# Second stage in two passes of four units, first batch's units ahead of the second product, and VectorE in GpSimd's place for early weight tiles

## The chip, the cores and the metric

The kernel runs on one core of a Trainium2 chip. The metric is the device time of one execution in microseconds. Of the core's engines TensorE (PE; its weight loads are shown as PEld) multiplies, VectorE (DVE) and ScalarE (ACT) work on tiles, GpSimd (POOL) does a part of the weight conversion, and SP issues most DMAs from one queue that is in order.

## The reference

Three layers in a row: an attention over 32 memory slots, a gated feed-forward (silu) and a feed-forward with an ELU.

```python
a = softmax(phi, axis=seq)                        # 8 batches, 8 heads, 576 x 32
k_m, v_m = a.T @ k, a.T @ v                       # 32 x 64 a head
attn = softmax(q @ k_m.T / 8)                     # 576 x 32
x = concat_heads(attn @ v_m)                      # 4608 tokens x 512
g, val = x @ w_gate, x @ w_val                    # 1536 columns each
x = (silu(g) * val) @ w_out                       # 4608 x 512
h = x @ w_in                                      # 2048 columns
out = where(h > 0, h, exp(min(h, 0)) - 1) @ w_out2
```

## The kernel before

**Numbers.** The weights come as 64-bit floats. `load_w` brings a tile of 128 x 512 of them to the chip (SP, 512 KB) and turns it into 32-bit floats: one ScalarE pass, four VectorE passes (L101, L102, L104, L105), and then GpSimd. With `split` (all `wo` and `w2` tiles) the tile becomes a high and a low half for products of three matmuls, with one ScalarE pass and two GpSimd passes (L108, L109); without (the `wg` tiles) one GpSimd pass (L111) adds the correction. After the first units exist, a conversion's VectorE passes are ordered behind the last one's `h` (L98).

**Stage one** (L392) goes over 8 batches, each in two halves of 288 tokens. The gate and value weights are multiplied with the batch's 32-slot `v_m` first: `vw(b, p)` (16 small matmuls, two ScalarE and two VectorE passes) makes the tile `VW[b, p]` for units 2p and 2p + 1, from four `wg` tiles of group p. A unit is 128 columns of the hidden layer: `gate1` (6 matmuls, L151 to L153), `val1` (6 matmuls, VectorE's `h` in L183, then halves `hh` and `hl` in L162 and L164). Stage one does units 0 to 3 (`UA = 4`); `down1` multiplies them with `wo` 0 to 3, four groups of 12 matmuls, and ScalarE stores the partial sum as `p1_d` in DRAM. Between the units, `tick()` issues pieces of a `todo` list in step with the number of ticks: the attention of later batches (`front_tasks`, `back_tasks`), weight tiles, and the next batch's `vw`. In the first batch these are the conversions of `wo` 0 to 3 and the attention of batches 1 and 2. In the last batch they are `load2(0)`, `wg` groups 4 and 5, `wo` 7 to 11, `vw(0, 2)` and `vw(0, 3)`. The attention result of each batch is also stored as `at_d`.

**Stage two** (L501) goes over the 8 batches again, two halves each, units 4 to 11 in each half. `at2` is read back from `at_d` (`load2`, two buffers). `down2` adds a unit into four PSUM banks `acc0` to `acc3` (one buffer each), two units late (`LAG = 2`). After the half's last unit VectorE adds the four banks to the tile `p1` that was read from `p1_d` (L475), and SP stores it as `x1_d`. The tile `p1` has one buffer, so the next half's `p1` is loaded when this store has landed. During hf 1 the four `vw` of the next batch are made, into four buffers of `vx`. 19 of the 32 `w2` tiles are converted here: one each in 11 halves, eight in the last batch.

**Stage three** (L577) goes over 9 blocks of 512 tokens with 16 units of 24 matmuls; the other 13 `w2` tiles are converted behind its first 13 units.

**Order.** All instructions are traced in this order, and a scheduler with a timeline model then sets the order on each engine's queue, earlier traced work first where both are ready in its model. `tc.issue_after(x)` keeps what is traced inside behind `x` on x's engine. On the chip each queue is in order.

Of the kernel before, what the change touches and what calls it, by code (L numbers as in the profile page):

```python
# [26 lines left out]
UA = 4  # L27
NCH = 5
NWA = 24
NWB = 16  # L30
NWE = 14
NWC = 10
NKV = 5
NQ = 3

# [2 lines left out]
def attention_moe_moe(ctx: ExitStack, tc: tile.TileContext, qT, phiT, kv, kv4, w1g, w1o, w2, out):  # L38
# [31 lines left out]

    at_d = [dram.tile([128, 2, 2, S], F32R, name=f"atd{b}") for b in range(B)]
    p1_d = [dram.tile([128, KD, S], F32, name=f"p1d{b}") for b in range(B)]
    x1_d = [dram.tile([128, KD, S], F32, name=f"x1d{b}") for b in range(B)]

    last = {}
# [7 lines left out]
                call()  # L83


    def load_w(store, u, i, src, pool, split=True):
        raw = wr_p.tile([128, 512, 2], I32, tag="wr", name="wr")
        nc.sync.dma_start(out=raw, in_=src.rearrange("p (n t) -> p n t", t=2))
        lo32, hi32 = raw[:, :, 0], raw[:, :, 1]
        if split:  # L90
            hi = pool.tile([128, 512], F32R, tag="w", name="whi")
            lo = pool.tile([128, 512], F32R, tag="w", name="wlo")
        else:
            full = pool.tile([128, 512], F32, tag="w", name="wg")
        v = wt_p.tile([128, 512], F32, tag="wv", name="wv")
        c = wt_p.tile([128, 512], I32, tag="wc", name="wc")
        vi, cf = v.bitcast(I32), c.bitcast(F32)
        with tc.issue_after(last["h"].ins) if "h" in last else nullcontext():  # L98

            act(out=v, in_=hi32.bitcast(F32), func=AF.Copy, scale=2.0 ** -112)  # L100
            nc.vector.tensor_scalar(out=c, in0=vi, scalar1=3, scalar2=None, op0=ALU.logical_shift_left)  # L101
            stt(out=vi, in0=vi, scalar=-2 ** 31, in1=c, op0=ALU.bitwise_and, op1=ALU.bitwise_or)  # L102

            nc.vector.tensor_scalar(out=c, in0=vi, scalar1=-2 ** 23, scalar2=None, op0=ALU.bitwise_and)  # L104
            stt(out=cf, in0=lo32.bitcast(U32), scalar=2.0 ** -52, in1=cf, op0=ALU.mult, op1=ALU.mult)  # L105
            if split:
                act(out=hi, in_=v, func=AF.Copy)
                nc.gpsimd.tensor_tensor(out=v, in0=v, in1=hi.bitcast(F32), op=ALU.subtract)  # L108
                nc.gpsimd.tensor_tensor(out=lo, in0=v, in1=cf, op=ALU.add)  # L109
            else:  # L110
                nc.gpsimd.tensor_tensor(out=full, in0=v, in1=cf, op=ALU.add)  # L111
        store[u][i] = (hi, lo) if split else full


# [4 lines left out]
    def load_wg(p, k, pool):  # L119
        load_w(WG, p, k, w1g[p, k], pool, False)  # L120

    def load_wo(u, pool):
        load_w(WO, u, 0, w1o[u], pool)

    def load_w2(u, i, pool):
        load_w(W2, u, i, w2[u, :, i * 1024:(i + 1) * 1024], pool)
# [19 lines left out]
    def up1(ps, w, c0, at, s0):  # L146
        cs, ss = slice(c0, c0 + 128), slice(s0, s0 + HS)
        for g in range(2):
            wh, wl = w[:, 0, g, cs], w[:, 1, g, cs]
            ah, al = at[:, 0, g, ss], at[:, 1, g, ss]  # L150
            mm(ps, lhsT=wh, rhs=ah, start=g == 0, stop=False)  # L151
            mm(ps, lhsT=wh, rhs=al, start=False, stop=False)  # L152
            mm(ps, lhsT=wl, rhs=ah, start=False, stop=g == 1)  # L153

    def down(ps, w, hs, ms, start, stop):
        mm(ps, lhsT=w[0][:, ms], rhs=hs[0], start=start, stop=False)  # L156
        mm(ps, lhsT=w[1][:, ms], rhs=hs[0], start=False, stop=False)  # L157
        mm(ps, lhsT=w[0][:, ms], rhs=hs[1], start=False, stop=stop)  # L158
# [208 lines left out]
    for k in range(KD):  # L367
        load_wg(1, k, wa_p)
    load(Bs[1])
    vw(0, 1, G2)  # L370

    def down1(b, hf, hs, m):
        ps = ps_gv.tile([128, HS], F32, tag="g", name="pd")
# [10 lines left out]
        at2[b] = av_p.tile([128, 2, 2, S], F32R, tag="at", name="at2")  # L384
        nc.sync.dma_start(out=at2[b].bitcast(F32), in_=at_d[b].bitcast(F32))


    def wg_tasks(p):
        return [lambda k=k: load_wg(p, k, wa_p) for k in range(KD)]

    prev = None
    for b in range(B):  # L392
        todo = []
        bk = list(back_tasks(b + 1)) if b + 1 < B else []
        fr = list(front_tasks(b + 2)) if b + 2 < B else []
        if b == 0:
            wo = [lambda u=u: load_wo(u, wa_p) for u in range(UA)]
            f1 = [lambda: (Bs[1].phi(), load_q(Bs[1]))] + list(front_tasks(1)) + [lambda: Bs[2].phi()]
            for i in range(max(len(wo), len(f1))):
                todo += wo[i:i + 1] + f1[i:i + 1]  # L400
        if 1 <= b <= 4:
            bk += [lambda k=k, p=2 + (b - 1) // 2: load_wg(p, k, wa_p) for k in (0, 1) if b % 2] + \
                [lambda k=k, p=2 + (b - 1) // 2: load_wg(p, k, wa_p) for k in (2, 3) if b % 2 == 0]
        if b == B - 2:
            wb_p = ctx.enter_context(tc.tile_pool(name="wb", bufs=NWB))
            ps_vw = ctx.enter_context(tc.tile_pool(name="ps_vw", bufs=1, space=PSUM))
            V2 = [(ps_vw, "vw"), (ps_gv, "g")]
            fr += [lambda u=u: load_wo(u, wb_p) for u in (4, 5, 6)]
        if b == B - 1:
            fr.append(lambda: load2(0))  # L410
            fr += wg_tasks(4) + [lambda: load_wo(7, wb_p), lambda: vw(0, 2, V2), lambda: load_wo(8, wb_p)]
            fr += wg_tasks(5) + [lambda: load_wo(9, wb_p), lambda: vw(0, 3, V2), lambda: load_wo(10, wb_p),
                                 lambda: load_wo(11, wb_p)]
        for i in range(max(len(bk), len(fr))):
            todo += fr[i:i + 1] + bk[i:i + 1]
        if b + 1 < B:
            todo += vw_tasks(b + 1)
        done = [0, 0]
        spread = 18 if b == 0 else 16 if b < B - 2 else 24

        def tick():
            done[0] += 1
            upto = min(len(todo), -(-len(todo) * (done[0] + 3) // spread))
            while done[1] < upto:
                todo[done[1]]()
                done[1] += 1

        silu = b == B - 1
        tick()
        for hf in range(2):  # L430
            hs = []
            for u in range(UA):
                s = gate1(b, u, Bs[b].at, HS * hf, silu)
                tick()
                hs.append(val1(b, u, Bs[b].at, HS * hf, s, silu))
                tick()
                if prev:
                    down1(*prev, u)
                    tick()
            prev = b, hf, hs  # L440
        while done[1] < len(todo):
            tick()
        if b == B - 3:
            st_fr.close()
            st_ps.close()
# [12 lines left out]
    def more_w2(pool, n=1):  # L458
        for _ in range(n):
            load_w2(*todo2.pop(0), pool)  # L460

    def load_p1(b, hf):
        t = p1_p.tile([128, KD, HS], F32, tag="p1", name="p1l")
        nc.sync.dma_start(out=t, in_=p1_d[b][:, :, HS * hf:HS * hf + HS])
        return t

    def down2(q):
        b, hf, u, hs, accs, p1 = q
        if u == UA:
            accs += [ps_acc.tile([128, HS], F32, tag=f"acc{m}", name=f"acc{m}") for m in range(KD)]  # L470
        for m in range(KD):
            down(accs[m], WO[u][0], hs, slice(128 * m, 128 * m + 128), u == UA, u == NU1 - 1)
        if u == NU1 - 1:
            for m in range(KD):
                tt(out=p1[:, m, :], in0=accs[m], in1=p1[:, m, :], op=ALU.add)  # L475
            nc.sync.dma_start(out=x1_d[b][:, :, HS * hf:HS * hf + HS], in_=p1)

    def load3(j):
        xt = []
# [14 lines left out]

    LAG = 2
    pend = []
    for p in (4, 5):
        vw(0, p, V2)
    w2q = [wa_p] * 4 + [we_p] * 7 + [wa_p] * 8
    vwq = []  # L500
    for b in range(B):  # L501
        for hf in range(2):
            p1 = load_p1(b, hf)
            accs = []
            if hf == 0 and b + 1 < B:
                load2(b + 1)
            for u in range(UA, NU1):
                s = gate1(b, u, at2[b], HS * hf, True)
                pend.append((b, hf, u, val1(b, u, at2[b], HS * hf, s, True), accs, p1))
                if len(pend) > LAG:  # L510
                    down2(pend.pop(0))
                if vwq:
                    vw(*vwq.pop(0), V2)
                if hf == 1 and u % 2 == 1 and b + 1 < B:
                    vwq.append((b + 1, u // 2))
                elif hf == 1 and u == 7 and b == B - 1:
                    nxt = load3(0)
                if u % 2 == 1 if b == B - 1 else u == 8 and len(w2q) > 8:
                    more_w2(w2q.pop(0))
    for q in pend:  # L520
        down2(q)
    pend = []
    st_p1.close()
    st_r.close()
    wc_p = ctx.enter_context(tc.tile_pool(name="wc", bufs=NWC, side="right"))
    w2q = [wb_p] * 8 + [wc_p] * 5
    h3_p = ctx.enter_context(tc.tile_pool(name="h3", bufs=4, side="right"))
    t3_p = ctx.enter_context(tc.tile_pool(name="t3", bufs=2, side="right"))

# [95 lines left out]
```

## Time and profile before

| | |
|---|---|
| median of 3 runs | 1608.3 us (1608.15 to 1608.68) |
| the profiled execution: own time, span | 1609.44 us, 1607.6 us |
| TensorE matmuls busy | 1533.4 us, 95% |
| VectorE busy | 988.0 us, 61% |
| ScalarE, GpSimd busy | 654.0 us, 166.2 us |
| mean granted TensorE clock | 0.981 |
| first matmul of stage one's first unit | 55.5 us |
| first matmul of stage two, last of it | 361.2 us, 810.0 us |

The span runs from the first to the last instruction; the own time has some 1.8 us around it. A busy TensorE is not one at its peak, since its matmuls are pipelined, so the windows below are read with their counts. The shares are means over stages that differ: in the first stage VectorE is nearly full at some places, in the second and third it is about half busy.

### The profile page before, as it was taken

The numbers are of one execution on the slowest core, as the hardware profiler recorded it, in microseconds if no ns is written. First come the engines' busy times: TensorE is split into PE (matmuls) and PEld (weight loads), VectorE is DVE, ScalarE is ACT, GpSimd is POOL, SyncE is SP. The second block draws the span as 40 slices with busy tenths as digits, with TensorE's granted clock in tenths as the row PEclk, the third lists the DMA queues.
The fourth block names the chain that finished last, engine by engine and source line by source line (L and its number), as shares of the span: only waits on it lengthen the run. The fifth ranks groups of instructions, "written<-read, shape, count | busy, mean of one in ns | idle before, by whom it ended". The sixth has DMA issues, their size and how long they took to land.

```text
span 1607.6 us, 24193 instructions
## 1 busy us (share of the span) xinstructions
PE 1533.4 (95%) x9816; PEld 1311.5 (82%) x9816; DVE 988.0 (61%) x1702; ACT 654.0 (41%) x1249; POOL 166.2 (10%) x119
## 2 busy tenths in 40 slices
PE   3599999979999999999998999999999999999998
PEld 2478789769999999999976788888888888888887
DVE  7997876795444454435889755555555555555554
ACT  3455444543333333333544433334343434343333
POOL 1400010241101011000435100000000000000000
PEclk7799999999999999999999999999999999999999
DMA  8887332452322232211522101001010101010000
GB/s 346 293 307 265 109 112 75 170 192 72 106 77 82 73 102 86 73 60 45 157 85 74 53 1 45 9 6 48 1 53 0 53 0 53 1 53 1 27 1 27
DMA packets 62961, 136.32 MB, mean 85 GB/s; under 512 B 6528, under 2 KB 37248, under 8 KB 60800
## 3 DMA queue, kind: packets, MB, share of 16 engines
q1 hardware_dynamic: 53632, 125.32, 22.7%
q10 hardware_dynamic: 9216, 9.44, 1.7%
q8 instruction: 77, 1.26, 0.3%
q14 instruction: 36, 0.29, 0.1%
HBM read 96.99 MB, written 37.75 MB: 84 GB/s over the span
## 4 chain that ended last, share of the span: by engine, by line
PE 81%; DVE 14%; DMA 2%; issue 2%; ACT 1%; SPq 0%; POOL 0%; ACTq 0%; DVEq 0%; POOLq 0%
PE acc L565 7%; PE acc L564 7%; PE acc L566 7%; PE pu L538 7%; PE pu L539 7%; PE pu L540 7%; PE acc L156 4%; PE acc L157 4%; PE acc L158 4%; PE pg L151 3%; PE pv L151 3%; PE pv L153 3%; PE pg L153 3%; PE pv L152 3%; PE pg L152 3%; PE pvw L139 3%
## 5 line engine op out<-in xcount | busy, mean ns | idle before, releaser
L538 PE MATMUL pu<-x1s,whi 128*128 128x512 f32 x576 | 224.7, 390 | 2.5 <-DVE g L554 2.5
L564 PE MATMUL acc<-whi,hh 128*128 128x512 f32 x576 | 224.5, 390 | 2.1 <-ACT hh L162 2.1
L566 PE MATMUL acc<-whi,hl 128*128 128x512 f32 x576 | 222.4, 390 | 3.3 <-DVE hl L164 3.3
L540 PE MATMUL pu<-x1s,wlo 128*128 128x512 f32 x576 | 224.8, 390 | 0.0
L539 PE MATMUL pu<-x1s,whi 128*128 128x512 f32 x576 | 224.7, 390 | 0.0
L565 PE MATMUL acc<-wlo,hh 128*128 128x512 f32 x576 | 224.2, 389 | 0.0
L553 DVE SCALAR_TENSOR_TENSOR g<-e,g 128x512 f32<-128x512 f32 x144 | 107.5, 747 | 157.5 <-ACT g L552 157.5
L162 ACT ACTIVATE hh<-g 128x512 fp32r<-128x512 f32 x144 | 91.0, 632 | 216.9 <-DVE g L554 216.9
L551 ACT ACTIVATE e<-g 128x512 f32<-128x512 f32 x144 | 90.8, 631 | 210.0 <-DVE g L550 210.0
L183 DVE SCALAR_TENSOR_TENSOR h<-s,pv 128x288 f32<-128x288 f32 x192 | 86.5, 451 | 140.8 <-PE pv L153 118.6
L164 DVE TENSOR_TENSOR hl<-g,hh 128x512 fp32r<-128x512 f32 x144 | 99.9, 694 | 88.3 <-ACT hh L162 88.2
L156 PE MATMUL acc<-hh,whi 128*128 128x288 f32 x512 | 151.0, 296 | 0.0
L157 PE MATMUL acc<-hh,wlo 128*128 128x288 f32 x512 | 150.6, 294 | 0.0
L158 PE MATMUL acc<-hl,whi 128*128 128x288 f32 x512 | 149.4, 295 | 0.0
L162 ACT ACTIVATE hh<-h 128x288 fp32r<-128x288 f32 x192 | 85.1, 443 | 138.9 <-DVE h L183 137.2
L164 DVE TENSOR_TENSOR hl<-h,hh 128x288 fp32r<-128x288 f32 x192 | 97.0, 505 | 63.0 <-ACT hh L162 62.8
L550 DVE TENSOR_SCALAR g<-pu 128x512 f32<-128x512 f32 x144 | 99.1, 689 | 55.2 <-PE pu L540 51.8
L566 PEld LDWEIGHTS acc<-whi,hl 128*128 128x128 f32 x576 | 108.0, 188 | 28.4 <-DVE hl L164 6.1
L151 PE MATMUL pg<-at,vw 128*128 128x288 f32 x384 | 119.4, 311 | 10.4 <-DVE vw L144 6.0
L564 PEld LDWEIGHTS acc<-whi,hh 128*128 128x128 f32 x576 | 108.3, 188 | 25.4 <-ACT hh L162 3.0
L538 PEld LDWEIGHTS pu<-x1s,whi 128*128 128x128 f32 x576 | 108.3, 188 | 25.3 <-DVE g L554 2.9
L539 PEld LDWEIGHTS pu<-x1s,whi 128*128 128x128 f32 x576 | 108.5, 188 | 22.6
(87 smaller groups left out, 3187.9 us busy)
## 6 DMA issues: line engine op xcount, KB each, us to landing
kvr<-kv SPq DMA_DIRECT2D x32, 512.0 KB, 7.9
wr<-w SPq DMA_DIRECT2D x32, 512.0 KB, 3.6
wr<-w1g SPq DMA_DIRECT2D x24, 512.0 KB, 4.9
qr<-qT SPq DMA_DIRECT2D x16, 576.0 KB, 5.9
atd<-at SPq DMA_DIRECT2D x8, 1152.0 KB, 5.3
p1d<-p ACTq DMA_DIRECT2D x64, 144.0 KB, 2.0
p1l<-p1d SPq DMA_DIRECT2D x16, 576.0 KB, 4.1
at<-atd SPq DMA_DIRECT2D x8, 1152.0 KB, 5.2
```

The lines of the kernel that those rows point to most:

```text
L151: mm(ps, lhsT=wh, rhs=ah, start=g == 0, stop=False)
L156: mm(ps, lhsT=w[0][:, ms], rhs=hs[0], start=start, stop=False)
L157: mm(ps, lhsT=w[1][:, ms], rhs=hs[0], start=False, stop=False)
L158: mm(ps, lhsT=w[0][:, ms], rhs=hs[1], start=False, stop=stop)
L162: act(out=hh, in_=h, func=AF.Copy)
L164: tt(out=hl, in0=h, in1=hh.bitcast(F32), op=ALU.subtract)
L538: mm(ps, lhsT=wh[:, k, :], rhs=xh, start=k == 0, stop=False)
L539: mm(ps, lhsT=wh[:, k, :], rhs=xl, start=False, stop=False)
L540: mm(ps, lhsT=wl[:, k, :], rhs=xh, start=False, stop=k == KD - 1)
L564: mm(accs[c], lhsT=hs[0][:, cs], rhs=wh, start=u == 0, stop=False)
L565: mm(accs[c], lhsT=hs[0][:, cs], rhs=wl_, start=False, stop=False)
L566: mm(accs[c], lhsT=hs[1][:, cs], rhs=wh, start=False, stop=u == NU2 - 1)
```

## The change

1. Stage two becomes two passes over all batches: units 4 to 7 with `p1_d` in and a new `p2_d` out, then units 8 to 11 with `p2_d` in and `x1_d` out. A half has four units; there are 32 halves instead of 16, `at` is read back 16 times instead of 8, and each batch of a pass needs two `vw`.
2. A list `conv` holds 34 conversions for stage two, one for each half (two in each of the last two): `wg` groups 4 and 5, `wo` 8 to 11, 22 `w2` tiles. The last batch of stage one keeps `wo` 7 only, and `vw(0, 4)`, `vw(0, 5)` are made during the first pass. Stage three converts 10 tiles. The pools' sizes follow (`NWB` 16 to 8, `NWE` 14 to 20, `NWC` 10 to 12).
3. `vw(0, 1)` is traced behind the first batch's second unit instead of ahead of the loop. In the first batch the `todo` list starts four ticks later (`-1` for `+3`), and what it issues on TensorE is kept behind the last `up1`.
4. In `load_w` the last additions run on VectorE instead of GpSimd for all `wg` tiles and for `wo` 0 to 3.

```diff
-                nc.gpsimd.tensor_tensor(out=v, in0=v, in1=hi.bitcast(F32), op=ALU.subtract)
-                nc.gpsimd.tensor_tensor(out=lo, in0=v, in1=cf, op=ALU.add)
+                part = tt if own else nc.gpsimd.tensor_tensor
+                part(out=v, in0=v, in1=hi.bitcast(F32), op=ALU.subtract)
+                part(out=lo, in0=v, in1=cf, op=ALU.add)
             else:
-                nc.gpsimd.tensor_tensor(out=full, in0=v, in1=cf, op=ALU.add)
+                tt(out=full, in0=v, in1=cf, op=ALU.add)
...
-        load_w(WO, u, 0, w1o[u], pool)
+        load_w(WO, u, 0, w1o[u], pool, own=u < UA)
...
-            mm(ps, lhsT=wl, rhs=ah, start=False, stop=g == 1)
+            last["pe"] = mm(ps, lhsT=wl, rhs=ah, start=False, stop=g == 1)
...
-    vw(0, 1, G2)
...
-            fr += wg_tasks(4) + [lambda: load_wo(7, wb_p), lambda: vw(0, 2, V2), lambda: load_wo(8, wb_p)]
-            fr += wg_tasks(5) + [lambda: load_wo(9, wb_p), lambda: vw(0, 3, V2), lambda: load_wo(10, wb_p),
-                                 lambda: load_wo(11, wb_p)]
+            fr += [lambda: load_wo(7, wb_p), lambda: vw(0, 2, V2), lambda: vw(0, 3, V2)]
...
-            upto = min(len(todo), -(-len(todo) * (done[0] + 3) // spread))
+            upto = min(len(todo), -(-len(todo) * (done[0] + (3 if b else -1)) // spread))
             while done[1] < upto:
-                todo[done[1]]()
+                with nullcontext() if b else tc.issue_after(last["pe"].ins):
+                    todo[done[1]]()
                 done[1] += 1
...
+                if (b, hf, u) == (0, 0, 1):
+                    vw(0, 1, G2)
...
+    conv = [lambda p=p, k=k: load_wg(p, k, wa_p) for p in (4, 5) for k in range(KD)] + \
+        [lambda u=u: load_wo(u, wa_p) for u in range(2 * UA, NU1)] + \
+        [lambda pool=pool: more_w2(pool) for pool in [we_p] * 10 + [wa_p] * 4 + [wb_p] * 4 + [wa_p] * 4]
...
+    for ps, (src, dst) in enumerate(((p1_d, p2_d), (p2_d, x1_d))):
+        for b in range(B):
+            nb, np_ = (b + 1, ps) if b + 1 < B else (0, ps + 1)
+            for hf in range(2):
+                p1 = load_p1(b, hf, src)
+                accs = []
+                if hf == 0 and np_ < 2:
+                    load2(nb)
+                for u in range(UA * (ps + 1), UA * (ps + 2)):
+                    s = gate1(b, u, at2[b], HS * hf, True)
+                    pend.append((b, hf, u, val1(b, u, at2[b], HS * hf, s, True), accs, p1, dst))
+                    if len(pend) > LAG:
+                        down2(pend.pop(0))
+                    if vwq:
+                        vw(*vwq.pop(0), V2)
+                    if hf == 1 and u % 2 == 1 and np_ < 2:
+                        vwq.append((nb, u // 2 + UA // 2 * (np_ - ps)))
+                    elif hf == 1 and u == 9 and np_ == 2:
+                        nxt = load3(0)
+                    if u % (2 if np_ == 2 else 4) == 1:
+                        conv.pop(0)()
...
-    w2q = [wb_p] * 8 + [wc_p] * 5
+    w2q = [wa_p] * 4 + [wc_p] * 6
```

## Rows read from the trace of the kernel before

**Rows 1.** The page's busy times, and TensorE in 40 slices of 40.2 us

```profile
PE 1533.4 (95%) x9816; PEld 1311.5 (82%) x9816; DVE 988.0 (61%) x1702; ACT 654.0 (41%) x1249; POOL 166.2 (10%) x119
...
PE   3599999979999999999998999999999999999998
```

**Rows 2.** Windows by stage; the columns stand in the first line

```profile
core 0: us, PE busy (x) PEld busy (x) DVE busy (x) ACT busy (x) POOL busy (x), PEclk, DMA share, GB/s
20.00:55.50 35.50, 15.17 (x159) 6.83 (x159) 35.09 (x60) 13.67 (x28) 10.64 (x8) 0.55 0.90 340
20.00:104.20 84.20, 54.58 (x602) 36.88 (x602) 83.23 (x154) 39.41 (x86) 19.77 (x14) 0.76 0.83 308
104.20:144.50 40.30, 39.21 (x441) 33.20 (x440) 31.28 (x67) 22.87 (x54) 2.56 (x2) 1.00 0.74 266
313.80:361.20 47.40, 38.31 (x298) 32.84 (x296) 45.77 (x69) 23.63 (x50) 21.35 (x15) 0.99 0.62 208
361.20:367.30 6.10, 6.06 (x27) 4.55 (x27) 5.85 (x8) 3.48 (x8) 3.70 (x4) 0.54 0.36 111
472.10:527.80 55.70, 55.70 (x451) 51.71 (x450) 26.18 (x57) 20.15 (x44) 6.29 (x4) 1.00 0.27 84
750.70:810.00 59.30, 59.30 (x443) 57.55 (x443) 45.03 (x85) 27.01 (x57) 22.65 (x16) 1.00 0.42 133
819.40:890.00 70.60, 65.40 (x272) 51.66 (x273) 69.51 (x96) 34.84 (x57) 36.82 (x24) 0.98 0.20 68
975.00:1060.00 85.00, 85.00 (x376) 70.38 (x375) 46.81 (x69) 33.08 (x53) 0.00 (x0) 1.00 0.08 25
```

**Rows 3.** Chain of waits in order of time: start us, us, what

```profile
395.35 1.02 PE pvw L139 x16
```

**Rows 4.** Waits of TensorE from 313.8 to 372 us: total, times, longest

```profile
PE pg L151 <- DVE vw L144: 5.7, 2, 3.5
...
PE pvw L139 <- ACT p L377: 1.4, 1, 1.4
```

**Rows 5.** VectorE's groups by line and shape, 367 to 750 us

```profile
L164 DVE TENSOR_TENSOR hl<-h,hh 128x288 fp32r<-128x288 f32 x111 | 51.7, 466 | 49.1 <-ACT hh L162 49.0
...
L475 DVE TENSOR_TENSOR p1l<-acc,p1l 128x288 f32<-128x288 f32 x52 | 21.2, 450 | 0.0
...
L102 DVE SCALAR_TENSOR_TENSOR wv<-wv,wc 128x512 int32<-128x512 int32 x11 | 7.6, 693 | 0.4
```

**Rows 6.** Timeline of VectorE at a change of half: start us, us

```profile
783.70 0.45 DVE L475 TENSOR_TENSOR p1l<-acc,p1l 128x288 f32<-128x288 f32 x1
...
786.60 0.45 DVE L475 TENSOR_TENSOR p1l<-acc,p1l 128x288 f32<-128x288 f32 x1
```

**Rows 7.** Timeline of SP's DMA queue, 410 to 430 us

```profile
414.95 0.33 SPq L385 DMA_DIRECT2D at<-atd  x1
...
424.92 0.55 SPq L476 DMA_DIRECT2D x1d<-p1l  x1
...
428.23 0.54 SPq L464 DMA_DIRECT2D p1l<-p1d  x1
```

**Rows 8.** DMA issues: KB each, median us from issue to landing

```profile
p1l<-p1d SPq DMA_DIRECT2D x16, 576.0 KB, 4.1
...
at<-atd SPq DMA_DIRECT2D x8, 1152.0 KB, 5.2
```

**Rows 9.** VectorE's groups by line and shape, 12 to 80 us

```profile
L102 DVE SCALAR_TENSOR_TENSOR wv<-wv,wc 128x512 int32<-128x512 int32 x12 | 11.9, 994 | 0.2
...
L164 DVE TENSOR_TENSOR hl<-h,hh 128x288 fp32r<-128x288 f32 x2 | 2.8, 1416 | 0.0
```

**Rows 10.** Timeline before the first unit: start us, us, what

```profile
34.29 0.65 DVE L144 TENSOR_TENSOR vw<-pvw,vw 128x512 fp32r<-128x512 f32 x1
...
35.34 0.76 DVE L308 TENSOR_TENSOR at<-ex,at 128x576 fp32r<-128x576 f32 x1
...
55.50 0.61 PE L151 MATMUL pg<-at,vw 128*128 128x288 f32 x1
```

## What was predicted, before the changed kernel ran

> **What bounds the kernel now.** I read the page first, then the windows by stage, then TensorE's waits in the windows where it is not full. TensorE is busy 1533.4 of 1607.6 us, and the digits of its slices fall below 9 at the left edge, in the ninth slice (322 to 362 us) and a little in the one from 844 us [rows 1]. So what there is to win stands in three places, and the rest has to stay as full as it is.
>
> The windows say how much [rows 2]. A batch of the steady second stage, 472.1 to 527.8 us, has TensorE at 55.70 of 55.70 us for 451 records, 448 by the code. Of these 64 are four `vw` products at 1.02 us each [rows 3], so 384 matmuls take 55.7 - 4.1 = 51.6 us, 0.134 us each; that is my yardstick for 288 columns. In the third stage 376 matmuls take 85.0 us, 0.226 us each.
>
> - *The last batch of stage one, 313.8 to 361.2 us.* VectorE is busy 45.77 of 47.40 us, TensorE 38.31. TensorE has 298 records; with four `vw` taken off (56 records are in the trace) some 242 matmuls are left. Work: 242 x 0.134 + 4 x 1.02 = 36.5 us. Lost: 10.9 us. In 361.2 to 367.3 the granted clock is 0.54, that is nearly all at the lower of its two levels (1.2 GHz, after the 3.5 us wait for `vw`), and 27 records that are worth at most 3.6 us take 6.1: another 2.5. What TensorE waits for is VectorE's `vw` [rows 4], which stands behind weight tiles 4 and 5 in VectorE's queue.
> - *The ramp of stage three, 819.4 to 890.* VectorE 69.51 of 70.60 us; 272 matmuls x 0.226 = 61.5 us, so 9.1 us are lost while 13 weight tiles are turned into halves, 0.70 us a tile.
> - *The start.* Between 20 and 104.2 us VectorE is busy 83.2 of 84.2 us and TensorE 54.6; the clock of 20 to 55.5 is 0.55.
>
> **The change, part by part.**
>
> *Tiles taken out of the last batch.* Eight `wg` tiles (groups 4 and 5), `wo` 8 to 11 and the products `vw(0,4)`, `vw(0,5)` leave the todo list of batch 7 and the lines behind it. Only `wo` 7, `load2(0)`, `vw(0,2)` and `vw(0,3)` stay. With VectorE no longer full, the batch should take what TensorE needs. Of 10.9 + 2.5 = 13.4 us I leave 1 for `wo` 7 and for hand-overs: -12.4 us. The two products are not saved, they run in stage two. Bounds: nothing, if another wait takes their place, and -13.4.
>
> *The same tiles in stage two.* All 34 conversions are now one a half (two a half in the last batch). VectorE is busy 26.18 of 55.70 us a batch there [rows 2], so it has 29 us free for each 55.7. It gets 15 tiles more than before (34 against 19) and 64 more additions of `p1` at 0.450 us [rows 5], 28.8 us. A tile's four passes take at most 4 x 0.69 = 2.8 us [rows 5], say 4 with what GpSimd's neighbourhood adds. That is some 90 us over eight old batches that have 236 free. Cost: 0 as long as that cover holds. The cover at the tight place, the change of half, is seen in the last old batch: there conversions, four additions and `load3` mix on VectorE, the additions end within 3.4 us [rows 6], and TensorE has 59.30 of 59.30 us in 750.7 to 810 [rows 2]. Without it, each late addition holds `acc0`, and the next `down2` waits behind it.
>
> *The doubled round of `p1`.* Each half is now 4 units, 4 x 24 x 0.134 = 12.9 us, and `p1` still has one buffer. The round is: additions (4 x 0.45 = 1.8 us), store, then the load that SP may issue only when the store has landed (3.3 us from issue to issue), then 4.1 us to landing [rows 7, 8]: 9.2 us against 12.9, so 3.7 us of slack where there were 16.5. SP gets 16 stores, 16 `p1` loads and 8 loads of `at` more. A store stands at the head of SP's queue until its additions are done, so the weight loads and the `at` load behind it wait too; each is asked for a half or more ahead. Cost 0; from the other side, if the 5.2 us of an `at` load [rows 8] came whole between store and reload, the round would be 14.4 us and a half would wait 1.5 us. The second pass reads `p2` 16 halves after it was stored, so nothing waits there.
>
> *Stage three.* 22 tiles are ready instead of 19, 10 remain: -3 x 0.70 = -2.1 us. Bounds 0 and -4, the latter if the last units catch up at the steady rate. The pools behind it (12 instead of 10 buffers in `wc`, still released by the last store) move nothing on the path. `load3(0)` is asked for two units before the end of the last half instead of four, but its `vx` buffers come free earlier; 0.
>
> *The start: VectorE's additions.* 16 GpSimd instructions of the first 100 us (one for each of 8 `wg`, two for each of 4 `wo`) become VectorE passes. The trace has no such pass; the nearest row is the two-input pass of the same size, 0.693 us [rows 5], so +11.0 us on a full engine. Against it: a VectorE pass beside a running GpSimd one is stretched. In 12 to 80 us the 12 passes of L102 mean 994 ns against 693 undisturbed, the two of L164 1416 against 466 [rows 5, 9]: 3.6 + 1.9 = 5.5 us from these two lines alone, which is the least, since others of its lines can be stretched in the same way. Net 0 to +5.5 us of VectorE, and each tile is ready sooner by GpSimd's longer time. I take +1 on the path, bounds -3 and +11.
>
> The Trainium skill, Perfetto Trace Analysis, section Optimizing Scalar/DVE Operations, advises moving work off a saturated VectorE, GpSimd included, which speaks against this edit; by that alone the sum would be 10 us worse. The same section adds that the two share a read port, so that moving between them might not help, and the stretched rows agree with that part.
>
> *The start: order.* `vw(0,1)` moves from ahead of the loop to behind unit 1, and the first batch's tasks start four ticks later, with their TensorE instructions behind the last `up1`. Now the first `pg` matmul runs at 55.50 us, behind the second `vw`, although the halves of `vw(0,0)` end at 34.9 and `at` at 36.1 [rows 10]. So two units, 24 matmuls, can move into a stretch in which TensorE idles: 3.2 us at 0.134, 6.4 at the lower clock. I take -5. Bounds: 0, if VectorE, which is full to 104 us, only trades this for a later batch 1; and the whole 19.4 us between 36.1 and 55.5, which VectorE could only pay for from its slack in batch 1 (31.28 of 40.30 us, 9 us free [rows 2]), so -10 is as far as I go. What waits behind: TensorE's queue is in order, so batch 1's transposes, products and scores, which VectorE waits for, stand behind the first `up1` until about 38 us.
>
> **Sum.** -12.4 - 2.1 + 1 - 5 = -18.5 us. The profiled execution's span is 1607.6 and its own time 1609.44 us, 1.1 above the median of 1608.3. So a span of 1589.1, an own time of 1590.9, a median of 1589.8; I say 1590.
>
> **The rivals.**
> 1. *The reload of `p1` becomes the bound (slower).* Place: every change of half in stage two. It decides once the round exceeds 12.9 us, and it costs more than the gain from 0.6 us a half on (18.5 over 31 halves). With the `at` load between store and reload in each of 16 batch passes it is 16 x 1.5 = 24 us, so 1590 + 24 = 1614. For it: one buffer, one queue. Against: the old `at` load went out at 414.95, ten us ahead of the store at 424.92 [rows 7].
> 2. *The start gets worse.* Deferred tasks make batch 1's attention late, or the 11 us of additions land on the path: +10 instead of -4, 1604. For it: VectorE has 1 us free in 84. Against: the stretched rows.
> 3. *The start gains far more*, as VectorE's slack of batches 1 and 2 is used: -14 instead of -4, 1580.
> 4. *The change doesn't do what it says for batch 7*: the batch stays slow, since the down products' copies (`p`, ACT) hold `ps_gv`; one 1.4 us wait of that kind stands beside 5.7 us of VectorE's [rows 4]. Half the 12.4 is lost: 1596.
>
> **How the numbers follow.** Forecast (1584 to 1595 of its own) 0.52; rival 3 0.15; rival 4 0.11; rival 2 0.11; rival 1 0.11. A difference under 0.2% (3.2 us) can't be told from none. Rival 1 is slower in most of its reach, and a bad case of 2 comes to no change: faster 0.85, same 0.04, slower 0.11. The range leaves out the far half of rival 3 and most of rival 1: 1577 to 1604.
>
> **What would show it.** Right: the last batch of stage one takes about 36 us with VectorE below half; stage two has TensorE full and 55.7 us for eight units' pairs; no wait of a `down2` on L475's additions; the first `pg` starts near 38 us and batch 1 near 99; the ramp shows 10 tiles. Wrong: `acc` matmuls waiting for additions or for `p1l` at the changes of half, a wait of `p1`'s additions on its load, low clock inside stage two, or batch 1 starting behind 104 us.

## The result, and the profile after

The changed kernel takes 1585.95 us (median of 4 runs, 1584.58 to 1587.06); the ratio to the kernel before is 0.9855, 95% interval 0.9838 to 0.9872. That is 22.5 us less, where 18.5 were forecast and the range was 1577 to 1604. The profiled execution has a span of 1584.9 us (own time 1587.06), 22.7 less than before. Where the 22.7 us stand, by the same marks in both traces:

| stretch | before, us | after, us | difference | forecast |
|---|---|---|---|---|
| first instruction to the first `pg` of batch 7 | 313.8 | 303.8 | -10.0 | -4 |
| batch 7, to the first `pg` of stage two | 47.4 | 34.4 | -13.0 | -12.4 with what follows |
| stage two, to its last `acc` matmul | 449.0 | 448.8 | -0.2 | 0 |
| the rest | 797.4 | 797.9 | +0.5 | -2.1 |

Some 2 of the 10.0 us at the start are not the change's. They stand in batch 3, which took 35.0 us before, with 6.8 us of it at TensorE's lower clock, and 32.9 after, without. Two traces of the experiments below (two buffers for `p1`, and late tasks only) have the same 6.8 us in that batch, and it takes 35.7 and 35.8 us there; with the whole start undone but no fall of the clock it takes 33.2. So this loss comes and goes from one execution to the next.

The page of the changed kernel, the lines that answer to [rows 1]: busy times, TensorE in 40 slices, and the granted clock.

```profile
PE 1523.7 (96%) x9816; PEld 1307.8 (83%) x9816; DVE 1013.3 (64%) x1798; ACT 649.6 (41%) x1249; POOL 113.4 (7%) x87
...
PE   4699999999999999999989999999999999999998
...
PEclk7899999999999999999999999999999999999999
```

The 7 in the ninth slice is gone. The edge at the left has a slice of 6 instead of 5, and the dip behind the stage change is still there. The windows, which answer to [rows 2]:

```profile
core 0: us, PE busy (x) PEld busy (x) DVE busy (x) ACT busy (x) POOL busy (x), PEclk, DMA share, GB/s
...
20.00:87.60 67.60, 45.57 (x457) 32.61 (x458) 65.21 (x137) 33.60 (x72) 0.00 (x0) 0.76 0.80 288
87.60:134.20 46.60, 42.58 (x495) 34.16 (x493) 41.49 (x92) 24.85 (x57) 0.00 (x0) 1.00 0.85 305
303.80:338.20 34.40, 34.40 (x275) 32.39 (x274) 11.97 (x25) 15.57 (x34) 3.12 (x2) 1.00 0.37 129
...
445.60:501.30 55.70, 55.70 (x450) 51.70 (x449) 37.32 (x72) 21.34 (x48) 10.46 (x8) 1.00 0.50 166
...
797.70:857.00 59.30, 55.08 (x223) 43.40 (x224) 58.21 (x79) 27.96 (x46) 30.87 (x20) 0.95 0.16 54
```

- Batch 7 (third row): VectorE 11.97 us where it had 45.77, TensorE full.
- Stage two (fourth row, two batches of a pass, the same work as one old batch): 55.70 us and 450 records as before; VectorE went from 26.18 to 37.32 us inside it and nothing of that shows.
- The ramp (last row): VectorE is full for 10 tiles now, and 59.3 - 223 x 0.226 = 8.9 us are lost, where 13 tiles had cost 9.1. The clock is part of both: 5.8 us of this window are at the lower level, worth up to 2.9 us, and 3.4 us of the window before, worth up to 1.7. That leaves 6.0 us for 10 tiles and 7.4 for 13, some 0.6 us a tile in both kernels.

The forecast's claim on VectorE's additions can be read off directly. VectorE's groups of the changed kernel in 12 to 80 us, which answer to [rows 5, 9]:

```profile
L103 DVE SCALAR_TENSOR_TENSOR wv<-wv,wc 128x512 int32<-128x512 int32 x12 | 8.1, 684 | 0.1
...
L166 DVE TENSOR_TENSOR hl<-h,hh 128x288 fp32r<-128x288 f32 x7 | 3.1, 450 | 0.4 <-ACT hh L164 0.4
...
L110 DVE TENSOR_TENSOR wv<-wv,whi 128x512 f32<-128x512 f32 x4 | 2.7, 682 | 0.0
```

L103 is the old L102: 684 ns instead of 994. L166 is the old L164: 450 instead of 1416. The added passes take 0.68 us each, as costed.

The round of `p1` in stage two was costed at 9.2 us. SP's queue in one short half (a half without `vw`), the median landing of the second pass's reloads and the landing of this one, and VectorE's first two additions behind it:

```profile
566.76 0.54 SPq L476 DMA_DIRECT2D p2d<-p1l  x1
569.13 0.33 SPq L89 DMA_DIRECT2D wr<-w  x1
570.69 0.55 SPq L463 DMA_DIRECT2D p1l<-p2d  x1
```
```profile
p1l<-p2d SPq DMA_DIRECT2D x16, 576.0 KB, 5.5
...
p1l<-p2d SPq DMA_DIRECT2D x1, 576.0 KB, 5.2
```
```profile
576.66 0.81 DVE L475 TENSOR_TENSOR p1l<-acc,p1l 128x288 f32<-128x288 f32 x2
```

Issue to issue is 3.9 us here (3.3 to 3.5 us at most of the other changes of half) and the landing 5.2 us: the tile is there at 575.9, 0.8 us ahead of the addition. Over the 14 changes that end a short half, the last one left out, the reload is 0.5 to 2.6 us early, 1.1 in the median; at the long ones it is 3.5 to 5.0 us early. Each term of the round but one is longer than costed: the four additions take 2.5 us instead of 1.8, and the landing is 5.3 us in the median of both passes instead of 4.1. With 3.4 us from issue to issue that is a round of 11.2 us, in a short half of 12.4.

At the end of stage two it isn't enough. The chain of waits of the changed kernel, start and length:

```profile
778.60 3.71 DMA x1d<-p1l
...
782.33 5.44 DMA p1l<-p2d
...
787.89 1.56 DVE p1l L475 x4
...
789.47 3.29 DMA x1d<-p1l
...
792.89 1.30 DVE g L553 x2
```

Behind the last unit no other unit's matmuls lengthen the half, so the additions wait 1.6 us for the reload. Then stage three's first `g` waits for the store, since its pool takes the memory that `p1` leaves. It did so in the kernel before, for as long (first line below, 3.42 us); what is new is the reload ahead of it. TensorE waits 4.9 us there, where it was 2.5 (second line before, third after):

```profile
814.59 1.29 DVE L550 TENSOR_SCALAR g<-pu 128x512 f32<-128x512 f32 x2 [3.42 <-DMA x1d<-p1l]
...
PE pu L538 <- DVE g L554: 2.5, 1, 2.5
...
PE pu L541 <- DVE g L557: 4.9, 1, 4.9
```

The clock falls to its lower level (1.2 GHz) there, for 6.8 us where it was 3.4. This difference is no sign of the change: of the six traces of experiments 1 and 2, whose code is the same at this place, three have 3.4 us and three 6.8.

### The profile page after: what moved, and what is told of

Read it like the earlier page. It is cut to its first block, busy times and chain, and to the rows that moved or that the text cites. A ratio compares the mean times of both kernels' runs of the same rounds, so it can differ in the third digit from the quotient of the medians.

```text
span 1584.9 us, 24325 instructions
## 1 busy us (share of the span) xinstructions
PE 1523.7 (96%) x9816; PEld 1307.8 (83%) x9816; DVE 1013.3 (64%) x1798; ACT 649.6 (41%) x1249; POOL 113.4 (7%) x87
## 4 chain that ended last, share of the span: by engine, by line
PE 84%; DVE 11%; DMA 3%; issue 1%; ACT 1%; SPq 0%; ACTq 0%; DVEq 0%
PE acc L567 8%; PE acc L568 8%; PE acc L569 8%; PE pu L543 8%; PE pu L541 8%; PE pu L542 8%; PE acc L158 4%; PE acc L160 4%; PE acc L159 4%; PE pg L153 3%; PE pv L153 3%; PE pg L155 3%; PE pv L155 3%; PE pv L154 3%; PE pg L154 3%; PE pvw L141 3%
## 5 line engine op out<-in xcount | busy, mean ns | idle before, releaser
L164 ACT ACTIVATE hh<-g 128x512 fp32r<-128x512 f32 x144 | 91.0, 632 | 216.1 <-DVE g L557 213.1
L166 DVE TENSOR_TENSOR hl<-g,hh 128x512 fp32r<-128x512 f32 x144 | 99.5, 691 | 90.0 <-ACT hh L164 89.9
L164 ACT ACTIVATE hh<-h 128x288 fp32r<-128x288 f32 x192 | 84.8, 442 | 125.5 <-DVE h L185 124.1
L166 DVE TENSOR_TENSOR hl<-h,hh 128x288 fp32r<-128x288 f32 x192 | 98.1, 511 | 52.3 <-ACT hh L164 52.3
L543 PEld LDWEIGHTS pu<-x1s,wlo 128*128 128x128 f32 x576 | 108.6, 189 | 22.4
```

The costliest lines, as they stand in the source:

```text
L164: act(out=hh, in_=h, func=AF.Copy)
L166: tt(out=hl, in0=h, in1=hh.bitcast(F32), op=ALU.subtract)
L543: mm(ps, lhsT=wl[:, k, :], rhs=xh, start=False, stop=k == KD - 1)
```

## The experiments

All are edits of the changed kernel; a time is the median, and the ratio is to the kernel before on the same chip. The changed kernel itself stands at 0.9855 (0.9838 to 0.9872).

**1. What made the start's gain: order or additions?** Three runs undo one, the other, and both.

```diff
@@ old order @@
+    vw(0, 1, G2)                        # ahead of the loop
...
-            upto = min(len(todo), -(-len(todo) * (done[0] + (3 if b else -1)) // spread))
+            upto = min(len(todo), -(-len(todo) * (done[0] + 3) // spread))
...
-                with nullcontext() if b else tc.issue_after(last["pe"].ins):
-                    todo[done[1]]()
+                todo[done[1]]()
...
-                if (b, hf, u) == (0, 0, 1):
-                    vw(0, 1, G2)
@@ additions on GpSimd @@
-                part = tt if own else nc.gpsimd.tensor_tensor
+                part = nc.gpsimd.tensor_tensor
...
-                tt(out=full, in0=v, in1=cf, op=ALU.add)
+                nc.gpsimd.tensor_tensor(out=full, in0=v, in1=cf, op=ALU.add)
```

Old order. 

> The changed kernel (1586.0 us) with the old order at the start: vw(0,1) ahead of the loop, the first batch's tasks four ticks earlier, nothing tied to the last up1; VectorE's additions stay. Theory A (the start's 10 us come from the order, since two units move into idle TensorE time): about 1594 to 1596. Theory B (they come from the additions, since VectorE is no longer stretched beside GpSimd): about 1586 to 1588, first pg still ahead of batch 1 by as much.

Additions on GpSimd. 

> The changed kernel with the last additions of wg tiles and of wo 0 to 3 back on GpSimd; the new order stays. Theory A: 1586 to 1588. Theory B: 1594 to 1596, VectorE's L103-type passes beside GpSimd at 1.6 us again.

Both undone. 

> Both undone at once: only the two passes and the moved tiles differ from the kernel before. If the parts add up, the last batch's 13 us are left: 1595 to 1597 under both theories. If the start's gain and the last batch's share something (the same VectorE backlog), it is off this by more than 3 us.

| | median, us | ratio | interval | first `pg` of batches 0, 1, 2, of stage two |
|---|---|---|---|---|
| changed kernel | 1585.95 | 0.9855 | 0.9838 to 0.9872 | 32.8, 87.6, 134.2, 338.2 |
| old order | 1592.42 | 0.9894 | 0.9881 to 0.9906 | 50.0, 102.7, 145.9, 346.6 |
| GpSimd adds | 1601.41 | 0.9941 | 0.9923 to 0.9959 | 35.2, 95.0, 146.0, 354.9 |
| both undone | 1593.42 | 0.9903 | 0.9890 to 0.9917 | 55.2, 103.9, 144.3, 345.8 |

Both theories fall. Against "both undone", the additions alone give nothing that can be told (0.9894 to 0.9903, intervals overlap), the order alone costs 0.38% (some 6 us), and the two together gain 0.48% (some 8 us). They are not two terms of a sum. What does add up is the last batch: with both undone it takes 34.3 us as in the changed kernel. No run puts the tiles back into that batch, so its cause rests on this and on VectorE's row there.

**2. Which half of the order, and which additions?** Three runs more.

```diff
@@ the product moved only @@
-            upto = min(len(todo), -(-len(todo) * (done[0] + (3 if b else -1)) // spread))
+            upto = min(len(todo), -(-len(todo) * (done[0] + 3) // spread))
...
-                with nullcontext() if b else tc.issue_after(last["pe"].ins):
-                    todo[done[1]]()
+                todo[done[1]]()
@@ the tasks late only @@
+    vw(0, 1, G2)                        # ahead of the loop
...
-                if (b, hf, u) == (0, 0, 1):
-                    vw(0, 1, G2)
@@ the additions of wo 0 to 3 on GpSimd @@
-                part = tt if own else nc.gpsimd.tensor_tensor
+                part = nc.gpsimd.tensor_tensor
```

The product moved only. 

> The changed kernel with vw(0,1) behind unit 1 as in the change, but the first batch's tasks four ticks earlier again and not tied to up1. If the moved product alone makes the start's gain: 1585 to 1588. If it needs the later tasks, so that they don't stand ahead of the units on TensorE: 1591 to 1594, as with the whole old order (1592.4).

The tasks late only. 

> The complement: vw(0,1) ahead of the loop again, the tasks late and tied as in the change. If the moved product makes the gain: 1592 or slower, since the tasks are late for nothing. If the late tasks make it: 1585 to 1588.

The additions of `wo` 0 to 3 alone on GpSimd. 

> The changed kernel with the additions of wo 0 to 3 alone back on GpSimd; those of the wg tiles stay on VectorE. With both on GpSimd it was 1601.4. If the new order needs the wg tiles of group 1 early (TensorE waits for the second vw in both), this stays at 1585 to 1589; if it needs the wo tiles early (down1 is late otherwise), it is 1594 to 1600.

Measured: moved product only 1593.04 us, 0.9909 (0.9891 to 0.9926), like the old order. Late tasks only 1586.18 us, 0.9857 (0.9842 to 0.9872), like the whole change. So the moved product alone shows no gain, although it brings the first `pg` to 32.8 us; the later tasks, with their TensorE instructions tied behind `up1`, give all of it. Whether the four ticks or the tie counts, no run separates. With `wo` on GpSimd: 1596.86 us, 0.9923 (0.9909 to 0.9937): of the two kinds of additions those of `wo` 0 to 3 carry most of what experiment 1 found (0.68 of 0.86%). The reason that was expected, late `wo` tiles, is not in the trace: the last of the four is finished at 65.8 us in both kernels, and the first `pd` matmul starts at 64.8 us, in the changed kernel at 65.3. What is in it are longer VectorE passes beside GpSimd's, in 12 to 80 us, where the changed kernel has 684 and 680 ns:

```profile
L106 DVE SCALAR_TENSOR_TENSOR wc<-wr,wc 128x512 f32<-128x512 uint32 x12 | 10.6, 893 | 0.1
L103 DVE SCALAR_TENSOR_TENSOR wv<-wv,wc 128x512 int32<-128x512 int32 x12 | 9.8, 824 | 0.1
```

The windows from 60 to 140 us show where the runs part. One row each of the changed kernel, late tasks only, old order, moved product only, `wo` on GpSimd, and all additions on GpSimd; the columns are those above, the last but two is the granted clock:

```profile
60.00:140.00 80.00, 74.53 (x950) 59.11 (x950) 72.12 (x157) 43.53 (x102) 0.00 (x0) 1.00 0.84 294
```
```profile
60.00:140.00 80.00, 73.71 (x948) 58.61 (x933) 74.03 (x160) 44.35 (x104) 0.00 (x0) 1.00 0.85 297
```
```profile
60.00:140.00 80.00, 71.70 (x843) 56.86 (x834) 68.49 (x147) 43.38 (x100) 0.00 (x0) 0.91 0.81 281
```
```profile
60.00:140.00 80.00, 68.46 (x800) 53.43 (x792) 69.17 (x149) 41.74 (x97) 0.00 (x0) 0.91 0.82 291
```
```profile
60.00:140.00 80.00, 74.15 (x830) 56.13 (x829) 66.16 (x142) 40.53 (x95) 3.71 (x3) 0.89 0.80 276
```
```profile
60.00:140.00 80.00, 73.81 (x809) 56.63 (x810) 68.46 (x141) 40.25 (x95) 9.79 (x7) 0.87 0.81 281
```

The first two get 950 and 948 TensorE records done and keep the full clock; the other four get 800 to 843, at a mean clock of 0.87 to 0.91. Read the busy column with care: `wo` on GpSimd shows TensorE as busy as in the changed kernel (74.15 against 74.53 us) with 120 records fewer, since the same matmul lasts longer at the lower level. A mean of 0.89 over 80 us is 2 x 0.11 x 80 = 17.6 us at the lower level, which takes up to 8.8 us; the first `pg` of batch 1 is 2.5 us later besides (90.1 against 87.6). At the first `pg` of batch 7 the run is 10.5 us behind, and 8 of these have come between 90 and 281 us, where GpSimd has nothing to do in either kernel. What TensorE did before the fall in that run: it stood 1.55 us ahead of a transpose, where the changed kernel stood 0.80 us at the same transpose, and 1.3 us after that wait the clock fell for 13.7 us.

```profile
109.98 0.44 PE L267 MATMUL ps_kvT<-ident,kvm 128*128 128x128 f32 x2 [1.55 <-DVE kvm L260]
```

That wait can't be called the cause. The run "both" of experiment 4 has the changed kernel's start. It stood 0.80 us at this transpose too, and its clock fell there all the same, for 6.8 us. Its row of the same window:

```profile
60.00:140.00 80.00, 77.20 (x952) 60.82 (x952) 72.55 (x158) 43.32 (x103) 0.00 (x0) 0.95 0.84 293
```

It got 952 records done and began batch 2 at 134.2 us, as the changed kernel did, and 1.1 to 1.7 us behind the five other runs with this start (132.5 to 133.1). So these 6.8 us at the lower clock cost it at most 1.7. No run changed the clock alone, and how much of the 10.5 us is clock and how much lateness stays open.

**3. How near is the round of `p1`?** One run gives it a second buffer, one makes the reload twice as long.

```diff
@@ two buffers @@
-    p1_p = st_p1.enter_context(tc.tile_pool(name="p1", bufs=1, side="right"))
+    p1_p = st_p1.enter_context(tc.tile_pool(name="p1", bufs=2, side="right"))
@@ reload twice @@
         nc.sync.dma_start(out=t, in_=src[b][:, :, HS * hf:HS * hf + HS])
+        nc.sync.dma_start(out=t, in_=src[b][:, :, HS * hf:HS * hf + HS])
```

Two buffers. 

> The changed kernel with two buffers for p1. Theory C (the round of p1 is hidden at every change of half but the last, where the additions wait 1.6 us for the reload and stage three starts that much later): -1 to -3 us, 1583 to 1585, and no wait of the additions on p1l. Theory D (the round costs nothing anywhere): 1586.

Reload twice. 

> The changed kernel with each load of p1 issued twice in a row, the second landing behind the first: 4.8 to 5.5 us more in the round. Theory C (the round fits a half by less than 1 us in the short halves): the additions wait at most changes of half and TensorE behind them, 2 to 3 us at 16 short halves and 0 to 1 at the others, 1620 to 1640. Theory D (far from the bound): within 3 us of 1586.

Two buffers: 1584.51 us, 0.9841 (0.9828 to 0.9854). The wait of the additions is gone from the trace and the way from the last `acc` to the second block of stage three is 88.7 us instead of 90.3. But the intervals overlap, and that way is 88.4 to 90.3 us in the seven traces that share the changed kernel's code there, so neither time tells. TensorE still waits 4.4 us for `g` in this trace, where the last store took 4.0 us instead of 3.3. Reload twice: 1652.11 us, 1.0268 (1.0252 to 1.0284), 66 us more than the changed kernel, worse than either theory had it. VectorE's and TensorE's waits in its stage two (total, times, longest):

```profile
DVE p1l L476 <- DMA p1l<-p1d: 39.1, 10, 6.2
...
DVE p1l L476 <- DMA p1l<-p2d: 25.0, 7, 5.9
```
```profile
PE acc L158 <- DVE p1l L476: 37.9, 21, 3.4
```

This is the forecast's rival 1, brought about on purpose: 5.5 us more in the round turn 22 us of gain into 43 of loss. Its place and its sign were right. By the forecast's own terms a round of 9.2 + 5.5 = 14.7 us in halves of 12.9 stalls 1.8 us at each of 31 changes, 56 us; measured are 66, or 2.1 at each in the mean. The round is not all of it: TensorE falls to the lower clock eight times in this stage two, 27 us together and worth up to 14, where it never does in the changed kernel, and the run also moves twice the bytes in reloads.

**4. Where did stage three's 2 us go?** One run gives the first `g` memory that `p1` does not hold, one spaces the 10 conversions, then both, then both with two buffers for `p1`.

```diff
@@ pools first @@
-    wc_p = ctx.enter_context(tc.tile_pool(name="wc", bufs=NWC, side="right"))
-    w2q = [wa_p] * 4 + [wc_p] * 6
...
+    wc_p = ctx.enter_context(tc.tile_pool(name="wc", bufs=NWC, side="right"))
+    w2q = [wa_p] * 4 + [wc_p] * 6
@@ spaced @@
-            if w2q:
+            if w2q and u % 3 != 2:
```

Pools. 

> The changed kernel with stage three's small pools (h3, t3) allocated ahead of wc, so that they take memory freed by h, t and at, not by p1. Theory E (between the stages VectorE's first g waits 3.4 us for p1's last store only because it takes p1's memory, and the lower clock behind that wait follows from it): the 4.9 us wait of pu goes and most of the 6.8 us at the lower clock, -4 to -7 us, 1579 to 1582. Theory F (g would wait for the additions or for PSUM anyway): 1585 to 1586.

Spaced. 

> The changed kernel with stage three's 10 tiles converted behind two of every three units instead of each of the first ten. Theory G (the ramp's loss is VectorE being full, 2.8 us of units and about 3.5 us of a tile against 5.45 us a unit): loss falls from about 8 us to 2, 1579 to 1581. Theory H, the prediction's reckoning (0.70 us for each tile wherever it stands): 1586.

Both. 

> Both of the two edits before. E and G together: 1573 to 1576. If only one of them holds: 1580.

Both, and two buffers for `p1`. 

> The changed kernel with the small pools first, the spaced conversions and two buffers for p1. With the last change of half still 1.5 us late by p1 in the two-edit version (1576.7): 1574 to 1576. If that wait is covered by other work: 1576 to 1577.

| | median, us | ratio | interval | last `acc` of stage two to block 2 of stage three, us |
|---|---|---|---|---|
| changed kernel | 1585.95 | 0.9855 | 0.9838 to 0.9872 | 90.3 |
| pools first | 1580.09 | 0.9820 | 0.9805 to 0.9835 | 85.0 |
| spaced | 1580.66 | 0.9824 | 0.9806 to 0.9841 | 83.4 |
| both | 1576.68 | 0.9802 | 0.9787 to 0.9817 | 80.0 |
| both, two `p1` | 1576.15 | 0.9791 | 0.9776 to 0.9807 | 78.7 |

Theory E holds. TensorE's wait for `g`, 4.9 us in the changed kernel and 2.5 in the one before, is this with the pools first, and no lower clock follows it (waits of TensorE, total, times, longest). The store held `g` in the kernel before too, so this gain is one that the change had not lost:

```profile
PE pu L541 <- DVE g L557: 1.3, 2, 0.7
```

Theory G holds against the prediction's own reckoning: the same 10 tiles, only spaced, and the ramp is full. The time alone is not clear of the changed kernel (0.9841 against 0.9838 at the edges); the last column is, 83.4 us against 88.4 to 90.3 in seven traces.

```profile
797.00:868.80 71.80, 71.80 (x310) 58.96 (x309) 62.84 (x91) 34.73 (x57) 30.91 (x20) 0.98 0.14 45
```

71.8 - 310 x 0.226 = 1.7 us lost, and the clock of 0.98 accounts for about that much, against 8.9 with up to 2.9 of it clock. The last two versions differ by less than their intervals; both beat the kernel before by some 2% and the changed kernel by 0.5 to 0.6%. The one with both edits came out 0.7 us slower than expected; its execution in the profile spent 6.8 us at the lower clock in batch 1, which the others of this group did not.

## Why the prediction was right, and where not

- *The last batch of stage one: right in mechanism and size.* -12.4 were forecast with the slow clock behind it; the batch lost 13.0 us of its length in the changed kernel and 13.1 with the start undone. VectorE was the wait, and nothing took its place: rival 4 did not come.
- *Stage two: right that it costs nothing, with less to spare than reckoned.* TensorE is full through all changes of half. VectorE's cover held (37.32 of 55.70 us). But the step "9.2 us against 12.9, so 3.7 us of slack" sized the additions and the landing by rows of before; the round became 11.2 us, and in the short halves 0.5 to 2.6 us were left. The run with the reload doubled shows that rival 1's mechanism was real.
- *Stage three: wrong.* Forecast were -2.1 us; the profile has +0.5, and the seven traces with the changed kernel's code there have 88.4 to 90.3 us from the last `acc` to the second block, against 89.8 before. The step that failed is that the pools behind it "move nothing on the path". It did not ask what the last, shorter half does: the reload came 1.6 us late, the store and the `g` that waits for its memory came later with it, and TensorE's wait grew from 2.5 us to 4.9 (4.2 to 5.3 in the other six). The step "-3 x 0.70 = -2.1" fared better than the sum: without the clock the two ramps differ by 1.4 us (7.4 and 6.0). But it took for a price of each tile what is the price of taking them one a unit on a full VectorE: spacing them gave back about 5 us with none removed.
- *The start: right sign, wrong reason, half the size.* The step "two units, 24 matmuls, can move into a stretch in which TensorE idles" is the one that failed. Moving the product alone shows no gain; the later tasks alone give all of it. The additions were booked as a small cost of +1 beside it; the runs show that the new order needs them: with the additions on GpSimd it is slower than the old one. The gain, some 8 us by the runs and by the profile without batch 3's clock, lies between the forecast's -4 and rival 3's -14, and a start that gets worse, rival 2, is what the new order gives as soon as GpSimd does the additions. Why it does stays open (experiment 2).
- *The advice against loading a full VectorE.* The Trainium skill, Perfetto Trace Analysis, section Optimizing Scalar/DVE Operations, has both sides: work may go from a full VectorE to GpSimd, but since the two share a read port that might not help. The runs agree with the second half. The passes added are 16 x 0.68 = 10.9 us, and VectorE is no longer stretched (684 ns against 994). With the old order no difference can be told; with the new one the move to VectorE is worth 0.86% (0.9855 against 0.9941).

That the total came within some 4 us of the forecast is in part luck: too much was expected of stage three and too little of the start, and the two errors have opposite signs.

## What to carry to other kernels

When two edits touch the same crowded stretch, don't add their prices: measure each with and without the other, since an order that leaves no slack can need the very edit that looks neutral alone. A conversion on a nearly full engine, like the one in the ramp here, has a rate that fits or does not, and a price per tile only while it does not; so spread it before removing any of it. When a loop's round is halved, recompute every single-buffered round with its slowest landing, and look at the last turn by itself, and at what next takes its memory.

## What the runs showed of the hardware

- The busy time of TensorE hid the clock: 77.20 us busy with 952 records at a mean clock of 0.95, 74.53 us with 950 at 1.00, and 74.15 us with 830 at 0.89, all in the same 80 us. Counts and the granted clock have to be read with it.
- The last wait ahead of a fall did not tell whether the clock falls. Behind the same transpose it fell for 13.7 us after a wait of 1.55 us, for 6.8 us after one of 0.80 us, and in the changed kernel, after 0.80 us, not at all.
- Landings of the same 576 KB were longer where there was more traffic: reloads took 4.1 us before [rows 8] and 4.8 (first pass) and 5.5 us (second) after, and the 1152 KB loads of `at` 7.0 instead of 5.2. A steady stretch of stage two moved 166 GB/s instead of 84.
